# Attention values in one call and w_in cast on chip, in a pooled-attention and GELU-product kernel

## The chip, the cores and the metric

The kernel runs on one core of a Trainium2 chip. The time is the device time of one execution in microseconds (us). Before the change, four runs have a median of 287.18 us (287.03 to 288.27). TensorE does the matrix products, VectorE, ScalarE and GpSimd (POOL) work on elements, SyncE (SP) issues transfers.

## The reference, cut to what matters

```python
q, k, v: (8 batches, 8 heads, 576 tokens, 64) float32
k_p = k.reshape(B, H, 72, 8, D).mean(axis=3)      # pool 8 tokens into one
v_p = v.reshape(B, H, 72, 8, D).mean(axis=3)
attn = softmax(q @ k_p^T / sqrt(D))                # 576 x 72 for each head
x = (attn @ v_p), heads side by side               # 4608 tokens x 512
h = x @ w_in                                       # 512 x 2048
out = gelu_tanh(h) @ w_out                         # 2048 x 512
```

## The kernel before, in words

Tokens are worked on in nine groups: batches 0 to 6 with 512 tokens each, then the remainder R (the last 64 tokens of every batch, 512 in all), then batch 7. A group has two parts. Its **attention** pools k and v over eight tokens (`pool`, L147 to L149; `spread_v`, L169, lays v out in `vbd` by a mask), makes scores (L229, L236), exponentials on ScalarE (`exps`, L244), sums and norms (`norm`, L251 to L263, into `eb`), transposes the normed weights into `eT` by DMAs on SP's queue (`e_transpose_dma`, L293), and multiplies them with the values into a PSUM tile `xo`, which is cast to bf16 as `xT` (512 rows of x in four blocks ko of 128 partitions, 512 tokens wide). Its **mlp** is a first product `w_in_b` x `xT` (four products for each of 16 column blocks fo, `hidden`, L380; GELU by ScalarE into `gT`) and a second product.

The mlp of one group and the attention of the next run together: the mlp goes through its TensorE instructions in a written order, and a dictionary of hooks says ahead of which of them a piece of the next group's attention is put. The first product is steps 0 to 63, the second 64 to 175. For groups behind the first, the second product is done by seven block products instead of eight (L471 to L508): sums of blocks of gT (`g_sums`, L431 to L434, into `stage`) and of w_out (`w_sums`, tile `tw`), then 7 x 16 = 112 products of 256 columns in the order 1, 2, 6, 5, 7, 3, 4. The PSUM bank x takes part 1, then 6, 7 and 4 on top; its state after each is kept as k2, k0, and so on (`x_copy`, `x_add`). The order in which a schedule is written is the order on each engine; nothing is rearranged.

There are four ways to make values:

- `values_half` (L298), for batch 0: 256 tokens and two of four head pairs in a call.
- `values` (L313), for batch 1 and, in the changed kernel, for all later groups: all 512 tokens. For a batch it splits each product over partitions 0 to 127 into pieces that touch only the rows and the 64 columns of one head, first the eight SMALL ones on 32 rows, then the eight BIG ones on 64 rows (L325), which add onto the same PSUM. For R (L334) it is 64 products of 64 columns.
- `values_part` (L340), for the groups behind batch 1: 256 tokens in a call, sixteen products of 256 columns in both calls together (L348), or twice 32 of 64 columns for R (L356). Its two `xo` tiles hold two blocks ko each and are copied by ScalarE and VectorE (128x512 each, L88 and L90). The first call is at step 64 + 92 of the mlp before, the second at step 4 of the group's own mlp (counted in full-size steps).
- Because of the two halves, the first four column blocks of those mlps are done in products of 256 columns, half of the tokens after the other (`hidden_half`, L391, GELU L393).

PSUM is split in two tags, "mm" with four banks and "sc" with two tiles of two banks (scores, values).

At the start, SP's queue carries k, q and v of batch 0 (L539 to L546), and `load_w_in` (L549) loads w_in in four DMAs on POOL's queue, which turn float32 into bf16 on the way: columns 0 to 1023 behind the exponentials of batch 0, the rest behind `spread_v`. A one-element DMA on SP's queue (L643) reads the second of these pieces, so that what follows on SP (k, q of batch 1, w_out in float32 to `w_out_s` and `stage`, v of batch 1; L644 to L653) comes behind it. w_out is cast by POOL and ScalarE (`cast_w_out`). `mlp_first` (L511) is batch 0's mlp: it begins with the first 256 tokens (half 0) of column blocks 0 to 7, has the last transposes of batch 0 as hooks at 16 and 28 (`first_t`, L289) and the values of the second 256 tokens at 32 (`first_v`, L304), and ends with a plain second product (`output`, L396).

Of the kernel before, what the change touches and what calls it, by code (L numbers as in the profile page):

```python
# [8 lines left out]
F32 = mybir.dt.float32  # L9
# [10 lines left out]
def kernel(  # L20
# [21 lines left out]
    nc = tc.nc  # L42
# [43 lines left out]
    def copy(eng, out, in_):  # L86
        if eng is nc.scalar:
            eng.copy(out=out, in_=in_)  # L88
        else:
            eng.tensor_copy(out=out, in_=in_)  # L90
# [221 lines left out]

    def values(g, eng):  # L313

# [21 lines left out]
        for i in range(2):  # L336
            copy(eng, st[g]["xT"].rearrange("p (y i) t -> p i y t", i=2)[:, i], xo[i])


    def values_part(g, half, engs):  # L340

        xo = [psum.tile([128, 2, 256], F32, name="xo", tag="sc", bufs=2) for _ in range(2)]
        eT = st[g]["eT"]
        for x in range(2):
            if g < B:
                for pr in (x, x + 2):
                    for y, (c, n) in enumerate(PARTS[pr]):
                        nc.tensor.matmul(out=xo[pr // 2][:, x, :], lhsT=vbd[:, g, n, :],  # L348
                                         rhs=eT[:, 2 * half:2 * half + 2, c, :], start=(y == 0), stop=(y == 1))
                continue  # L350
            for pr in (x, x + 2):
                for b in range(4 * half, 4 * half + 4):
                    p0 = 64 * (b % 2)
                    t0 = 64 * (b - 4 * half)
                    for y, (c, n) in enumerate(PARTS[pr]):
                        nc.tensor.matmul(out=xo[pr // 2][:, x, t0:t0 + 64], lhsT=vbd[:, b, n, :],  # L356
                                         rhs=eT[:, b // 2, c, p0:p0 + 64], start=(y == 0), stop=(y == 1))
        for k in range(2):
            copy(engs[k], st[g]["xT"][:, 2 * k:2 * k + 2, 256 * half:256 * half + 256], xo[k])

# [74 lines left out]

    def mlp(g, hooks, last, split):
        hook = runner(hooks)
        if split:
            for half in range(2):
                for fo in (0, 2):  # L440
                    hidden_half(g, fo, half, lambda s: hook(s // 2) if s % 2 == 0 else None, 16 * half + 4 * fo)
        for fo in range(4 if split else 0, FO):
            hidden(g, fo, hook, 4 * fo)
# [30 lines left out]
        for n, (prod, acc, fresh) in enumerate([(1, xs, 1), (2, y, 1), (6, xs, 0), (5, z, 1), (7, xs, 0), (3, z, 0), (4, xs, 0)]):  # L474
# [17 lines left out]
            if prod == 1:  # L492
                x_copy(nc.vector, k2)
            elif prod == 6:
                x_copy(nc.scalar, k0)
            elif prod == 5:
                copy(nc.scalar, k1, z)
                add(out=k2, in0=y, in1=k2, op=ALU.add)
            elif prod == 7:
                x_add(k1, k1)  # L500
                if last:
                    store_pair(g, 1, osb[1], HN, DM)
            elif prod == 3:
# [101 lines left out]
    for j in range(2):  # L605
        scores(0, j)
        exps(0, j)
    load_w_in(0)
    load_w_in(1)
    pool(0, 5, 7)  # L610
# [5 lines left out]
    spread_v(0, nc.gpsimd, (2,))  # L616
    load_w_in(2)
    load_w_in(3)
# [12 lines left out]
    nc.scalar.preload_act_table_set(GELU_SET)  # L631
    norm(0, 2, nc.vector)
    norm(0, 3, nc.vector)

    def first_t(j):
# [6 lines left out]

    nc.sync.dma_start(out=gate[0:1], in_=w_in_b[0:1, 0, 512:513])  # L643
    kv_tile(1)  # L644
# [72 lines left out]
    for n_, g in enumerate(seq):  # L717
# [12 lines left out]
        if n_ + 1 < len(seq):  # L730
# [48 lines left out]
        if 2 <= n_ <= 5:  # L779
            at(hooks, 58, load_q, R, n_ - 2, n_ - 1, nc.sync)  # L780
        mlp(g, hooks, n_ + 1 == len(seq), n_ > 1)

# [29 lines left out]
```

## Time and profile before

| | |
|---|---|
| median of 4 runs | 287.18 us |
| profiled execution, its own time | 287.12 us |
| its span, first to last instruction | 285.4 us |
| granted TensorE clock | 1.00 |
| TensorE busy | 276.7 us, 97% |
| VectorE busy | 206.1 us, 72% |
| ScalarE busy | 166.7 us, 58% |
| POOL busy | 58.4 us, 20% |
| one pass of the main loop on TensorE (95.64 to 124.46) | 28.82 us |
| w_in, four DMAs of POOL, issued 9.58 to 16.34 | landed 15.53, 18.03, 21.49, 25.53 us |
| first product of batch 0 begins | 17.82 us |

The profile gives a busy time for each engine, the idle time in front of an instruction with what ended it, and a chain of waits followed back from the last instruction. Matrix products are pipelined: the time of one (0.38 us with 512 columns) is longer than the distance between two (0.216). A few records of TensorE are missing, so a gap of exactly one product is no wait.

### The profile page before, as it was taken

Reading aid. Unit: us, or ns where it says so; the run is one execution under the profiler, and the core shown is the slowest. Engines: PE = TensorE matmul, PEld = TensorE weight load, DVE = VectorE, ACT = ScalarE, POOL = GpSimd, SP = SyncE. Lnnn points to the kernel's source line nnn. Section 1 sums busy time; section 2 is a strip of 40 time slices with the busy share of each in tenths; the row PEclk is TensorE's granted clock in tenths of the full one; section 3 lists DMA queues with packets and bytes.
Section 4 is the critical chain, followed back from the end, with each engine's and each line's share of the span. In section 5 each row is a group of like instructions: output and inputs, shape, how many; then the busy total and the mean of one; then the engine's idle time right before and its main releaser. Section 6 shows DMA issues by size and latency. Waiting matters only on the chain.

```text
span 285.4 us, 5568 instructions
## 1 busy us (share of the span) xinstructions
PE 276.7 (97%) x2193; PEld 198.0 (69%) x2203; DVE 206.1 (72%) x377; ACT 166.7 (58%) x262; POOL 58.4 (20%) x91
## 2 busy tenths in 40 slices
PE   8889999999999999999999999999999999999994
PEld 3678854447884788478846984698468956985583
DVE  5882869989858985898589948994899345944521
ACT  1586574796457744775467547754785367536510
POOL 4730363003300340033003300331032100100000
PEclk9999999999999999999999999999999999999999
DMA  7999999999999997797979977936713530253003
GB/s 229 305 192 290 375 385 190 328 300 274 198 253 265 348 133 189 213 328 130 172 220 334 125 155 216 263 72 155 193 68 67 144 106 2 49 111 82 2 2 148
DMA packets 71357, 54.31 MB, mean 190 GB/s; under 512 B 45602, under 2 KB 57378, under 8 KB 71330
## 3 DMA queue, kind: packets, MB, share of 16 engines
q1 hardware_dynamic: 69218, 51.85, 70.7%
q0 software_dynamic: 2112, 2.10, 4.6%
q8 instruction: 17, 0.28, 0.4%
q14 instruction: 10, 0.08, 0.2%
HBM read 36.70 MB, written 9.44 MB: 162 GB/s over the span
## 4 chain that ended last, share of the span: by engine, by line
PE 82%; DMA 8%; DVE 7%; issue 1%; SPq 1%; POOL 0%; DVEq 0%
PE mm L485 32%; PE mm L380 29%; PE mm L391 10%; DMA w_out_s<-in_moe_w_out_dram 5%; PE xo L348 4%; PE x L485 2%; PE sc L229 2%; DMA kv<-in_v_dram 2%; DMA qT<-q_b 2%; DVE den L251 1%; DVE eb L263 1%; PE mm L396 1%; DVE kv L147 1%; DVE eb L278 1%; DVE kv L148 1%; PE xo L356 1%
## 5 line engine op out<-in xcount | busy, mean ns | idle before, releaser
L380 PE MATMUL mm<-xT,w_in_b 128*128 128x512 bf16 x392 | 87.4, 379 | 0.4
L382 ACT ACTIVATE gT<-mm 128x512 bf16<-128x512 f32 x100 | 59.7, 598 | 25.0 <-PE mm L380 24.9
L380 PEld LDWEIGHTS <-w_in_b 128*128 128x128 bf16 x400 | 39.1, 98 | 45.9 <-issue 0.3
L485 PEld LDWEIGHTS <-gT 128*128 128x128 bf16 x512 | 49.3, 98 | 7.1
L169 POOL TENSOR_TENSOR vbd<-kvb,vmask 128x256 bf16<-128x256 bf16 (+2 forms) x40 | 23.8, 616 | 92.6 <-DVE kvb L149 92.4
L391 PE MATMUL mm<-xT,w_in_b 128*128 128x256 bf16 x352 | 42.3, 273 | 0.1
L485 PEld LDWEIGHTS <-stage 128*128 128x128 bf16 x384 | 37.2, 98 | 4.2
L391 PEld LDWEIGHTS <-w_in_b 128*128 128x128 bf16 x352 | 34.1, 98 | 4.2 <-issue 0.2
L393 ACT ACTIVATE gT<-mm 128x512 bf16<-128x512 f32 x44 | 26.1, 597 | 14.7 <-PE mm L391 14.7
L90 DVE CAST xT<-xo 128x512 bf16<-128x512 f32 x16 | 11.1, 692 | 29.1 <-PE xo L348 23.5
L485 PE MATMUL mm<-w_out_b,gT 128*128 128x256 bf16 x240 | 30.8, 273 | 0.0
L244 ACT ACTIVATE e<-sc 128x576 f32<-128x576 f32 x36 | 22.5, 650 | 11.4 <-PE sc L229 6.6
L88 ACT COPY osb<-mm 128x512 f32<-128x512 f32 x23 | 13.5, 587 | 26.2 <-PE mm L485 26.2
L485 PE MATMUL mm<-tw,gT 128*128 128x256 bf16 x240 | 28.7, 273 | 0.0
L251 DVE TENSOR_REDUCE den<-e 128x8 f32<-128x576 f32 x36 | 26.4, 735 | 2.3 <-ACT e L244 2.3
L485 PE MATMUL mm<-tw,stage 128*128 128x256 bf16 x224 | 27.9, 273 | 0.0
L147 DVE TENSOR_TENSOR kv<-kv 128x1024 f32<-128x1024 f32 (+3 forms) x19 | 21.0, 1106 | 6.5 <-DMA kv<-in_k_dram 5.2
L431 DVE TENSOR_TENSOR stage<-gT 128x512 bf16<-128x512 bf16 (+1 forms) x31 | 16.2, 522 | 13.1 <-ACT gT L382 7.8
L88 ACT CAST xT<-xo 128x512 bf16<-128x512 f32 (+1 forms) x18 | 11.3, 634 | 18.9 <-PE xo L348 11.1
L263 DVE TENSOR_TENSOR eb<-e,r 128x576 bf16<-128x576 f32 x24 | 20.5, 855 | 0.8
L432 DVE TENSOR_TENSOR gT<-gT 128x512 bf16<-128x512 bf16 (+1 forms) x31 | 14.6, 470 | 6.6 <-ACT gT L382 5.1
L263 POOL TENSOR_TENSOR eb<-e,r 128x576 bf16<-128x576 f32 x6 | 6.9, 1151 | 52.6 <-ACT e L244 52.6
(84 smaller groups left out, 295.5 us busy)
## 6 DMA issues: line engine op xcount, KB each, us to landing
kv<-in_k_dram SPq DMA_DIRECT2D x7, 1024.0 KB, 6.9
q_sb<-in_q_dram SPq DMA_DIRECT2D x7, 1024.0 KB, 11.2
out_dram<-osb SPq DMA_DIRECT2D x13, 512.0 KB, 3.0
kv<-in_v_dram SPq DMA_DIRECT2D x6, 1024.0 KB, 8.9
kv<-in_v_dram SPq DMA_DIRECT2D x4, 512.0 KB, 10.1
w_in_b<-in_moe_w_in_dram POOLq DMA_DIRECT2D x4, 512.0 KB, 6.7
w_out_s<-in_moe_w_out_dram SPq DMA_DIRECT2D x2, 1024.0 KB, 13.5
stage<-in_moe_w_out_dram SPq DMA_DIRECT2D x2, 1024.0 KB, 14.5
```

Of the source, the lines that this page charges most:

```text
L88: eng.copy(out=out, in_=in_)
L147: add(out=t[:, :, 0:4, :], in0=t[:, :, 0:4, :], in1=t[:, :, 4:8, :], op=ALU.add)
L169: eng.tensor_tensor(out=vbd[p0:128, b, n0:n1, :].rearrange("p (c r) (hh d) -> p c (r hh) d", c=max(m, 1), d=D), in0=kvb[p0:128, 4 + c0:4 + ...
L244: nc.scalar.activation(out=e.rearrange("p (x h) s -> p x (h s)", x=2), in_=sc[:, :, 0:4 * Sp], func=ACT.Exp, scale=1.0 / 64.0)
L251: nc.vector.reduce_sum(out=den, in_=e, axis=AX.X)
L263: eng.tensor_tensor(out=o.rearrange("p (h s) -> p h s", s=Sp), in0=e, in1=r.unsqueeze(2).to_broadcast([128, H, Sp]), op=ALU.mult)
L380: nc.tensor.matmul(out=hp, lhsT=w_in_b[:, ko, fo * 128:(fo + 1) * 128], rhs=st[g]["xT"][:, ko, :], start=(i == 0), stop=(i == KO - 1))
L382: nc.scalar.activation(out=gT[:, fo, :], in_=hp, func=ACT.Gelu_apprx_tanh)
L391: nc.tensor.matmul(out=hp[:, f, :], lhsT=w_in_b[:, ko, (fo + f) * 128:(fo + f + 1) * 128], rhs=st[g]["xT"][:, ko, c0:c0 + 256], start=(ko ...
L393: nc.scalar.activation(out=gT[:, fo:fo + 2, c0:c0 + 256], in_=hp, func=ACT.Gelu_apprx_tanh)
L431: nc.vector.tensor_tensor(out=s3, in0=a11, in1=a21, op=ALU.subtract)
L485: nc.tensor.matmul(out=xs[p] if acc is xs else acc[:, p, :], lhsT=lt, rhs=rt, start=bool(fresh and m == 0 and (p == 0 or (last and acc is ...
```

## The change

It has four parts.

1. For batches 2 to 7 and R the two calls of `values_part` are gone. `values` is called once for all 512 tokens, at step 64 + 105 of the mlp before, and its two PSUM tiles are copied by ScalarE (blocks ko 0 and 2) and VectorE (blocks 1 and 3), 128x1024 each. For batch 1 both copies stay on ScalarE.
2. Those mlps no longer work in halves. Their first two column blocks are done by `hidden_two`, which takes the four products that need only the first copy ahead of the four others; the rest are `hidden`. This holds for batch 1's mlp too, which had no halves before.
3. The copy k2 after part 1 of the second product goes from VectorE to ScalarE.
4. w_in is loaded by eight DMAs of 512 KB in float32 on SP's queue, directly behind batch 0's last load, into a second kv buffer and `stage`. VectorE casts two pieces, POOL ten. The gate DMA is gone; w_out's loads wait for the casts that read their buffers.

```diff
-    def values(g, eng):
+    def values(g, engs):
...
         for i in range(2):
-            copy(eng, st[g]["xT"].rearrange("p (y i) t -> p i y t", i=2)[:, i], xo[i])
-
-
-    def values_part(g, half, engs):
...
+            copy(engs[i], st[g]["xT"].rearrange("p (y i) t -> p i y t", i=2)[:, i], xo[i])
...
+    def hidden_two(g, hook):
+
+        hp = [psum.tile([128, MAIN], F32, name="mm", tag="mm", bufs=4) for _ in range(2)]
+        for s, (f, ko) in enumerate([(0, 0), (0, 2), (1, 0), (1, 2), (0, 1), (0, 3), (1, 1), (1, 3)]):
+            hook(s)
+            nc.tensor.matmul(out=hp[f], lhsT=w_in_b[:, ko, f * 128:(f + 1) * 128], rhs=st[g]["xT"][:, ko, :],
+                             start=(ko == 0), stop=(ko == 3))
+        for f in range(2):
+            nc.scalar.activation(out=gT[:, f, :], in_=hp[f], func=ACT.Gelu_apprx_tanh)
+
+    def mlp(g, hooks, last):
         hook = runner(hooks)
-        if split:
-            for half in range(2):
-                for fo in (0, 2):
-                    hidden_half(g, fo, half, lambda s: hook(s // 2) if s % 2 == 0 else None, 16 * half + 4 * fo)
-        for fo in range(4 if split else 0, FO):
+        hidden_two(g, hook)
+        for fo in range(2, FO):
             hidden(g, fo, hook, 4 * fo)
...
             if prod == 1:
-                x_copy(nc.vector, k2)
+                x_copy(nc.scalar, k2)
...
     nc.scalar.preload_act_table_set(EXP_SET)
-
-    def load_w_in(c):
-        nc.gpsimd.dma_start(out=w_in_b[:, :, 512 * c:512 * c + 512],
-                            in_=moe_w_in[:, 512 * c:512 * c + 512].rearrange("(ko p) f -> p ko f", p=128))
+    w_in_s = []
+    for c in range(4):
+        if c % 2 == 0:
+            w_in_s.append(kvp.tile([128, KO, 1024], F32, name="w_in_s", tag="kv") if c == 0 else
+                      stage.rearrange("p (k f) -> p k f", k=KO))
+        o = 512 * (c % 2)
+        for k0 in (0, 2):
+            nc.sync.dma_start(
+                out=w_in_s[-1][:, k0:k0 + 2, o:o + 512],
+                in_=moe_w_in[128 * k0:128 * k0 + 256, 512 * c:512 * c + 512].rearrange("(ko p) f -> p ko f", p=128))
+
+    def cast_w_in(c, k0, eng, f0=0, f1=512):
+        o = 512 * (c % 2)
+        copy(eng, w_in_b[:, k0:k0 + 2, 512 * c + f0:512 * c + f1], w_in_s[c // 2][:, k0:k0 + 2, o + f0:o + f1])
...
     e_transpose_pe(0, 1, nc.vector, "mm")
+    cast_w_in(0, 2, nc.vector, 0, 256)
     scores(0, 2)
     exps(0, 2)
     for x in range(2):
         values_half(0, 0, x, [nc.vector, nc.scalar][x], "mm")
     scores(0, 3)
+    cast_w_in(0, 2, nc.vector, 256, 512)
     sums(0, 2)
     exps(0, 3)
     nc.scalar.preload_act_table_set(GELU_SET)
     norm(0, 2, nc.vector)
     norm(0, 3, nc.vector)
+    cast_w_in(0, 0, nc.gpsimd)
+    for c in range(1, 4):
+        cast_w_in(c, 0, nc.gpsimd)
+        cast_w_in(c, 2, nc.gpsimd, 0, 256)
+        cast_w_in(c, 2, nc.gpsimd, 256, 512)
...
-    nc.sync.dma_start(out=gate[0:1], in_=w_in_b[0:1, 0, 512:513])
...
-        at(hooks, va, values, n, nc.scalar)
+        at(hooks, va, values, n, [nc.scalar, nc.scalar])
...
-            at(hooks, 64 + 92, xT_tile, n)
-            at(hooks, 64 + 92, values_part, n, 0, [nc.scalar, nc.vector])
-        if n_ > 1:
-            at(hooks, 4, values_part, g, 1, [nc.scalar, nc.vector])
+            at(hooks, 64 + 105, xT_tile, n)
+            at(hooks, 64 + 105, values, n, [nc.scalar, nc.vector])
```

The calls of `load_w_in` are taken out as well; nothing else in the schedule moves.

More of the change, by code (lines that the diff above doesn't have):

```diff
@@ L336, in values @@
         for i in range(2):
-            copy(eng, st[g]["xT"].rearrange("p (y i) t -> p i y t", i=2)[:, i], xo[i])
-    def values_part(g, half, engs):
[L342 to L359, printed above, removed]
+            copy(engs[i], st[g]["xT"].rearrange("p (y i) t -> p i y t", i=2)[:, i], xo[i])
     def store(g, r, osb, c0=0, c1=DM, eng=nc.sync):
@@ L434, in g_sums @@
         nc.vector.tensor_tensor(out=s4, in0=a12, in1=s2, op=ALU.subtract)
-    def mlp(g, hooks, last, split):
-        hook = runner(hooks)
-        if split:
-            for half in range(2):
-                for fo in (0, 2):
-                    hidden_half(g, fo, half, lambda s: hook(s // 2) if s % 2 == 0 else None, 16 * half + 4 * fo)
-        for fo in range(4 if split else 0, FO):
+    def hidden_two(g, hook):
[7 more added lines that the diff above has]
+    def mlp(g, hooks, last):
+        hook = runner(hooks)
+        hidden_two(g, hook)
+        for fo in range(2, FO):
             hidden(g, fo, hook, 4 * fo)
@@ L607 @@
         exps(0, j)
-    load_w_in(0)
-    load_w_in(1)
     pool(0, 5, 7)
@@ L616 @@
     spread_v(0, nc.gpsimd, (2,))
-    load_w_in(2)
-    load_w_in(3)
     norm_two(0, 1, 5)
@@ L780 @@
             at(hooks, 58, load_q, R, n_ - 2, n_ - 1, nc.sync)
-        mlp(g, hooks, n_ + 1 == len(seq), n_ > 1)
+        mlp(g, hooks, n_ + 1 == len(seq))
 _INS = ['q', 'k', 'v', 'moe_w_in', 'moe_w_out']
```

## The prediction

> **What bounds the kernel.** I read the page first, its busy shares and its chain.
>
> ```profile
> PE 276.7 (97%) x2193; PEld 198.0 (69%) x2203; DVE 206.1 (72%) x377; ACT 166.7 (58%) x262; POOL 58.4 (20%) x91
> ...
> PE 82%; DMA 8%; DVE 7%; issue 1%; SPq 1%; POOL 0%; DVEq 0%
> ```
>
> TensorE works for 276.7 of 285.4 us, and 82% of the chain of work that ended last is TensorE. A change is worth what it takes from TensorE's order or adds to it; other engines count where they make TensorE wait. Then the chain in order of time, for one pass of the main loop (95.5 to 125 us; columns are start, length, piece):
>
> ```profile
> 106.68 0.87 PE xo L348 x8
> 107.55 2.18 PE mm L485 x20
> 109.74 0.87 PE mm L391 x8
> 110.61 0.87 PE xo L348 x8
> 111.48 2.62 PE mm L391 x24
> ```
>
> The values of a batch cost 2 x 0.87 us here: eight products of 256 columns between the second product's steps (L348), eight more inside the next first product. No piece waits. (The 112 products of a pass's second product are numbered 0 to 111.) A pass is 28.82 us (95.64 to 124.46, the same piece twice). The operation that replaces these rows runs once before, for batch 1 (timeline from 48.8 us; start, length, instruction, the wait before it):
>
> ```profile
> 49.01 1.81 PE L325 MATMUL xo<-eT,vbd 32*64 32x512 bf16 x16
> ...
> 50.65 1.93 ACT L88 CAST xT<-xo 128x1024 bf16<-128x1024 f32 x2 [4.30 <-PE xo L325]
> ...
> 50.75 1.47 PE L396 MATMUL mm<-w_out_b,gT 128*128 128x512 bf16 x6
> ```
>
> Sixteen products of 512 columns, on 32- and 64-row parts of the array, are over in 1.74 us (49.01 to 50.75) although they wait for vbd twice; full-size products of 512 columns pass at 0.216 us each (46 in 10.09 us), sixteen at 3.46. So the parts overlap.
>
> **1. Values in one call.** Taken one by one, the last four small products begin together but for one that waits until 49.86; the large ones begin in two groups of four at 50.19 and 50.41; TensorE goes on at 50.75. A group of four therefore costs 0.22, and each change of tile size adds about 0.1 (50.19 less 49.86 is 0.33; 50.75 less 50.41 is 0.34). Four groups at 0.22 and three changes at 0.1 are 1.2 us. Before: 16 x 0.109 = 1.74. Saving 0.54 in each of the six calls for batches 2 to 7 that move. If small groups of different i didn't overlap at 0.22 but at 0.33, 0.3 of it is lost. For the remainder (L356) count and width of the products stay: nothing. The first four column blocks of the first product go from 32 x 0.109 = 3.49 to 16 x 0.216 = 3.46: 0.03 in seven passes. The Trainium skill speaks against the change here: TensorEngine Tiling (Array Packing), Key Properties, says that a change of tiling mode drains TensorE. The rows have it at 0.1 a change; were each a full drain of the visible 0.4 us of such a product, the call would cost 2.1 and the sum be 5 us worse.
>
> **2. The new wait for xT.** Before, other products lie between a value product and its use. Now seven products of the second product remain behind the values (105 to 111): 7 x 0.109 = 0.76. The row of batch 1 gives the copy: ScalarE starts at 50.65, 0.1 before TensorE leaves the values, and two copies of 128x1024 take 1.93, one 1.01. First copy ready 0.97 after the values (with 0.06 to release), TensorE there after 0.76: **stall 0.21**. ScalarE has nothing ahead: table load at 104.26 to 105.54, next copy 107.37. The order (0,0), (0,2), (1,0), (1,2) gives 4 x 0.216 = 0.86 before the VectorE half is needed, at 1.83. VectorE has no copy of 128x1024 from PSUM; 256 elements take 0.42, 512 take 0.69, so 1.24 by the step (bounds 0.69 and 2 x 0.69). It starts 0.55 before ScalarE's end, hence is ready at 1.4 (1.6 at worst): hidden, cover 0.4. Ahead of it VectorE has the addition L504, which starts 0.25 after product 96 and takes 0.68, over before the values end. Behind it wait pool and k of the next batch, which before began 4 us after this point and now 3. The remainder has its first block done 0.93 earlier, no stall. In batch 1 the order removes a wait of 0.14 (52.63).
>
> Per pass: -0.54 - 0.03 + 0.21 = -0.36; times six is **-2.1**; remainder -0.03; batch 1 -0.14.
>
> **3. All four transposes of e at once.** Before, values at product 92 needed j = 0, 1, and j = 2, 3 only 3.9 us later. Now all four are needed at product 105: 106.52 + 13 x 0.109 = 107.94, or 136.76 one pass on. SP's timeline there, and the row of the tile eT (issue to landing):
>
> ```profile
> 129.38 5.99 SPq L293 DMA_TRANSPOSE eT<-eb  x4
> ```
>
> ```profile
> DMA to landing us min/median/max: 2.6/2.6/3.0
> ```
>
> The last of the four is issued at 134.15; with 2.6 it lands at 136.75, right at the edge. What decides is the copy of k2, which leaves VectorE (timeline from 126 us):
>
> ```profile
> 126.95 0.68 DVE L90 COPY osb<-mm 128x512 f32<-128x512 f32 x1
> 127.55 0.74 DVE L251 TENSOR_REDUCE den<-e 128x8 f32<-128x576 f32 x1
> ```
>
> Sums of j = 0 start at 127.55, but the exponentials are done at 127.1, and work ahead of the copy ends at 127.0. So the chain (sum, reciprocal, norm, three more) moves 0.44 forward, and with it the transposes, as SP has no other work in between. Margin 0.44; in the pass at 72 us the last lands at 79.66, 0.5 earlier 79.15, needed 79.0. I charge 0.1 for the first passes together. On ScalarE, k2 (0.59) fits: exponentials end at 98.77, k2 would end at 99.36, product 6 overwrites x from 99.72, scores j = 2 come at 99.54. Cover 0.3; without it the excess is paid in each pass.
>
> **4. The start.** Four DMAs with cast on POOL's queue and the one-element gate go. Eight DMAs of 512 KB of f32 go on SP's queue behind q; their casts go to VectorE (2 of 512 elements, 0.43) and POOL (4 of 1024 at 1.04, 6 of 512 at 0.62). q lands at 13.26; w_out, in the same 2 KB rows, comes at 1024 KB in 2.70 (34.93 to 37.63). So 512 KB each 1.35 us after about 13.1: pieces of columns 0-511 at 14.4 and 15.8, the last at 24. VectorE wants its piece at 16.4, POOL at 15.5, TensorE starts at 17.82: no delay, cover 0.6. Before, the four landed at 15.53, 18.03, 21.49, 25.53; later columns are needed at 19.6, 23.2, 26.7 and cast by 19.8 (its second half is used at 20.5), 23.4, 25.7. Everything behind on SP (kv and q of batch 1, then w_out, which waits for the casts out of its buffers until 20 and 24 to 26) lands 1 to 1.7 earlier. POOL is through by 25.7; q of batch 1 and w_out, next on it, come at 30 and 33. That ends this stall of TensorE (0.39 by the starts, of which the timeline from 30 us lists 0.23):
>
> ```profile
> 35.65 0.81 PE L396 MATMUL mm<-w_out_b,gT 128*128 128x512 bf16 x3 [0.23 <-POOL w_out_b L90]
> ```
>
> Against it stands VectorE. Its second cast (0.43) stands ahead of sums j = 2, and the two norms behind (L263) meet POOL's casts. What that does (timeline from 37 us):
>
> ```profile
> 37.68 2.03 POOL L90 CAST w_out_b<-w_out_s 128x1024 bf16<-128x1024 f32 x2 [0.54 <-DMA w_out_s<-in_moe_w_out_dram]
> ...
> 38.81 1.50 DVE L263 TENSOR_TENSOR eb<-e,r 128x576 bf16<-128x576 f32 x1
> ...
> 41.25 0.76 DVE L263 TENSOR_TENSOR eb<-e,r 128x576 bf16<-128x576 f32 x1
> ```
>
> The same norm takes 0.76 alone and 1.50 beside POOL's casts. With casts at most 1.04 apart I take 0.3 of waiting for the cast and each norm: 0.43 + 0.3 in front of eb j = 2, 0.3 more for j = 3. TensorE wants both, in front of products 16 and 28, and first_v after: **+1.0** (bounds 0.45 with no meeting; 1.7 with both norms at 1.50). The Trainium skill, SBUF — State Buffer, Who interferes with whom, has GpSimd and a VectorE operation with two SBUF inputs exclude each other for a whole instruction; by that alone, up to 1.04 for each of three, the start would lose up to 3.1 instead of 1.0. The row agrees with waiting, and its 0.74 is what I use.
>
> At 49 us batch 1's values wait for vbd, the end of exponentials, four norms, pool and spread. That chain starts 1.0 later, but the norm of 1.50 above now runs after POOL's earlier casts: -0.74. So vbd comes +0.26; TensorE (1.0 - 0.39 = +0.61) is there before it either way. **Start: +0.26** (bounds -0.3 and +0.9).
>
> **The sum.** -2.1 - 0.03 - 0.14 + 0.1 + 0.26 = -1.9 us. The profiled execution took 287.12 with a span of 285.4; the median of four runs is 287.18, so the two agree. Prediction 285.2. This measurement tells a change from none at about 0.3%, 0.86 us.
>
> **Rivals.**
> *The transposes land late* (ends slower). Place: the first small value product of each pass, waiting for the fourth transpose. Longer landings are seen: 4.4 us (pass at 95 us, first of four, beside loads). Its 2.6 plus margin 0.44 is covered; beyond 3.4 us the wait exceeds the 0.36 gained. At 4.4 it is 1.35 late, six times 8.1: 293.3. For it: the window has no slack. Against: the fourth landed in 2.6 in every pass of the loop where it is recorded. 0.10.
> *The start eats the gain.* Both norms and the cast fully held, 1.7 instead of 1.0, and vbd not earlier (the norm still meets casts, +0.74): start +1.7 instead of 0.26, 286.6. For it: POOL casts 10 times in 10 us. Against: they wait for data in between. 0.14.
> *w_in late.* Loads cover 0.6. At 1.6 us per 512 KB, as q and v landed beside other traffic, the first pair lands at 16.3, just in time; if the queue holds it 2 us longer, TensorE starts 1.4 later, 286.6. Against: SP is free at 5.4, data are queued from then. 0.06.
> *More than I count.* Start at its good bound and no wait for xT: 285.2 - 0.56 - 1.26 = 283.4. 0.10.
> *The change doesn't overlap* (value parts one behind another, 3.46): +2.26 six times, 298.8. Row 49.01 excludes nearly all of it; part of the 0.10 of the first rival at most.
> Forecast, 284.4 to 286.2: 0.60.
>
> Faster (below 286.3): 0.60 + 0.10 and a fifth of the two middle ones, 0.74. Same (286.3 to 288.0): 0.15. Slower: 0.11. The range takes the good case at half, 283.9, and the start that eats the gain with small waits for transposes, 287.2.
>
> **What would show it.** Chain: values of a pass in one piece of about 1.2 us, no pieces of 256-column first product, a gap of 0.2 in front of the first product put down to ScalarE's copy; passes of 28.46. If the gap is put down to VectorE, the second copy is what I mis-sized. A gap in front of the values from a DMA on eT is the first rival. At the start, TensorE at first_v at 23.3 instead of 22.29, and norms of over 1 us. A first product after 18 us means w_in. Wrong altogether if passes stay at 28.8.

## The result and the profile after

| | before | after |
|---|---|---|
| median | 287.18 us (79 runs, 286.66 to 288.94) | 286.73 us (53 runs, 285.58 to 290.06) |
| ratio to before, 95% interval | | 0.9978 [0.9969, 0.9986] |
| profiled execution, its own time | 287.12 us | 287.41 us |
| its span | 285.4 us | 285.7 us |

The change gains 0.22% (0.63 us by the ratio), less than the 0.3% that the prediction gives as the least this measurement tells from none; 0.7% was forecast. One execution of after (290.06 us) and one of experiment 6 (576.0 us) were slow ones, and the ratios leave them out. The profiled execution of after lies 0.68 above its median, so its waits are probably larger than the usual ones. First the page of after: busy time, the instruction queue, and the chain that ended last, by engine and by line.

```profile
PE 273.3 (96%) x2074; PEld 178.8 (63%) x2091; DVE 203.4 (71%) x363; ACT 168.8 (59%) x264; POOL 62.5 (22%) x97
...
q8 instruction: 16, 0.26, 0.4%
...
PE 86%; DMA 7%; DVE 3%; SPq 2%; issue 1%
PE mm L359 32%; PE mm L471 30%; PE mm L420 5%; PE mm L375 5%; PE mm L370 4%; DMA w_in_s<-in_moe_w_in_dram 3%; PE xo L325 3%; DMA eT<-eb 3%; PE sc L229 3%; PE x L471 2%; DMA qT<-q_b 2%; DVE eb L263 1%; SPq L541 1%; DVE w_in_b L90 1%; SPq L108 1%
```

TensorE's busy time fell by 3.4 us and the span didn't. Two pieces stand in the chain that the prediction gave little room: 3% of the span on a transpose (`DMA eT<-eb`), and VectorE's norms (`eb L263`) and its cast (`w_in_b L90`) at the start. A pass without trouble, from the chain of after in order of time (start, length, piece):

```profile
137.49 1.11 PE xo L325 x16
138.60 0.87 PE mm L471 x7
139.47 0.03 issue
139.50 0.38 PE mm L420
```

The values cost 1.11 us in one piece. The last of the seven products behind them starts at 139.20, so the first product could start 0.109 later, at 139.31; it starts at 139.50, 0.19 late. The same chain two passes on:

```profile
191.16 3.55 DMA eT<-eb
194.71 0.14 issue
194.84 1.18 PE xo L325 x16
```

Here the last transpose, issued at 191.16, lands 3.55 later and TensorE stands idle for 0.53 in front of the values. There are three such waits: 0.55 (values at 108.97), 0.53 (194.84) and 0.84 (253.29). Where the time went, pass by pass (from the start of one second product to the next, in us of the span; the first row ends at the first scores of batch 2, so batch 1's first product, with its -0.14, lies in it):

| | before | after | difference | prediction |
|---|---|---|---|---|
| start, to the first scores of batch 2 | 66.94 | 67.84 | +0.90 | +0.12 |
| to 96 (a wait of 0.13 in before) | 28.70 | 28.19 | -0.51 | -0.36 |
| to 125 (wait 0.55) | 28.82 | 29.00 | +0.18 | -0.36 |
| to 153 | 28.83 | 28.44 | -0.38 | -0.36 |
| to 182 | 28.83 | 28.45 | -0.37 | -0.36 |
| to 211 (wait 0.53) | 28.82 | 28.98 | +0.16 | -0.36 |
| to 240, the remainder's values | 29.16 | 29.16 | 0.00 | -0.03 |
| to 269 (wait 0.84) | 28.83 | 29.29 | +0.46 | -0.36 |
| the rest | 16.47 | 16.35 | -0.12 | 0 |
| sum | 285.4 | 285.7 | +0.3 | -1.9 |

(The sum of the last column has 0.1 for the transposes; its terms are -1.97, put down as -1.9.) Two terms of the sum are off in this execution: the start by 0.8, and three waits of 1.92 together in place of 0.1. The row to 96 is 0.15 better than forecast because before, too, waited there for a transpose: it landed at 77.56, and the values began 0.13 late, at 77.69.

**What makes the transposes late.** Traffic of the DMA engines in 40 slices of 0.1 us, after, from 191 us (the row of GB/s, the instruction queue, and the transposes' median from issue to landing):

```profile
GB/s 51 187 218 223 212 202 223 190 100 23 8 166 0 31 131 205 223 189 210 179 100 26 8 10 10 8 10 8 10 151 132 0 0 0 0 0 0 0 0 0
...
q8 instruction: 1, 0.02, 1.6%
...
eT<-eb SPq DMA_TRANSPOSE x2, 4.0
```

And the pass that doesn't wait, from 133 us:

```profile
GB/s 233 210 218 212 223 195 80 10 0 0 0 33 164 220 233 200 228 210 200 131 21 0 0 0 18 136 218 225 207 228 212 205 157 34 0 0 0 0 0 0
...
eT<-eb SPq DMA_TRANSPOSE x2, 2.6
```

A transpose moves for 0.9 us at about 200 GB/s and is over. In the first window the traffic falls behind 193.1 to 8 to 10 GB/s for 0.7 us, then a last piece goes, and the transposes land after 4.0 (median) instead of 2.6. What is there and not in the second window is a 16 KB transfer of the instruction queue: it starts at 192.13 (the slice of 166 GB/s) and takes 1.02, to 193.15. The thin tail begins as it ends, and its rate is about a twentieth of the full one. I read this so: one of the 16 DMA engines was held by the transfer and works off its share alone, and a transpose isn't landed until its last share is. (The trace doesn't name the engine of a packet, so this reading of the rates and times is not shown.) There are 16 such transfers in the span, for 2074 + 2091 TensorE instructions, one in 260. The Trainium skill, Runtime: NRT & Kernel Launch, Instruction fetch mechanics, says that an engine's instructions are refilled in blocks of 16 KiB, 256 of them, over a DMA queue of its own, and that the cost of crossing such a block is mostly hidden. Size and spacing agree with the rows here; the cost here falls on another transfer.

In the three passes of after that wait they start at 104.59, 192.13 and 250.67, beside the later transposes. In the passes at 195 and 253 the third and the fourth land late (4.25 to 4.64 and 3.55 to 3.80). In the pass at 109 the second and the third do (4.35 and 3.56); SP issues the fourth 1.0 later than in other passes, and it lands in 2.57. A fourth pass is hit as well, the remainder's (a transfer at 220.79; 4.49 and 3.63), but the first of its products that reads the last block comes 0.35 behind its first one, and it waits only 0.05. The traces of all 14 runs say the same of the loop (passes behind 60 us, fourth transposes whose landing is recorded): 37 had a transfer between issue and landing and took 2.84 to 4.06 us, 3.53 in the median; 54 had none and took 2.58 to 3.01, 2.60 in the median.

The trace of before had such transfers too. Its window from 133 us:

```profile
GB/s 223 215 215 185 56 2 0 0 76 213 221 219 205 205 152 21 0 0 12 279 201 207 209 182 68 4 0 0 0 0 6 8 8 10 8 10 35 195 0 0
...
q8 instruction: 1, 0.02, 1.8%
```

The same picture in slices of 0.125 us: a transfer from 135.39 to 136.81, then the thin tail of 8 to 10 GB/s to 137.5, for a transpose issued at 134.15. It cost nothing there, since the second half of the values began at 139.27. The change took that cover away. (The old cover wasn't complete: in the profile of experiment 2, with values in two calls, a transfer of 2.04 us at 103.94 lies beside the first two transposes, which take 6.09 and 4.52, and the values at 107.94 wait 0.65, probably for them.)

**The start.** The chain of after from 17 us (it stands for this execution, see experiments 2 and 6):

```profile
17.56 1.22 DVE w_in_b L90
...
19.71 0.90 DVE eb L263
...
21.54 1.46 DVE eb L263
...
24.09 1.03 PE xo L304 x8
```

VectorE sets the end here: its cast took 1.29 (timeline; 0.41 alone), the norms 0.90 and 1.45 (0.76 alone). TensorE waits 1.16 and 0.79 for them, and `first_v` is at 24.09 instead of 22.29. POOL's side of it, from the timeline (start, length):

```profile
17.46 1.04 POOL L90 CAST w_in_b<-w_in_s 128x1024 bf16<-128x1024 f32 x1 [0.78 <-DMA w_in_s<-in_moe_w_in_dram]
```

POOL's cast began at 17.46, VectorE's at 17.49; VectorE ended at 18.78, 0.28 behind POOL's end. The norm at 21.54 stands behind a cast of POOL from 21.34 in the same way.

### The profile page after: what moved, and what is told of

It reads as the page before. It is cut to its first block, busy times and chain, and to the rows that moved or that the text cites. A ratio compares the mean times of both kernels' runs of the same rounds, so it can differ in the third digit from the quotient of the medians.

```text
span 285.7 us, 5348 instructions
## 1 busy us (share of the span) xinstructions
PE 273.3 (96%) x2074; PEld 178.8 (63%) x2091; DVE 203.4 (71%) x363; ACT 168.8 (59%) x264; POOL 62.5 (22%) x97
## 4 chain that ended last, share of the span: by engine, by line
PE 86%; DMA 7%; DVE 3%; SPq 2%; issue 1%
PE mm L359 32%; PE mm L471 30%; PE mm L420 5%; PE mm L375 5%; PE mm L370 4%; DMA w_in_s<-in_moe_w_in_dram 3%; PE xo L325 3%; DMA eT<-eb 3%; PE sc L229 3%; PE x L471 2%; DMA qT<-q_b 2%; DVE eb L263 1%; SPq L541 1%; DVE w_in_b L90 1%; SPq L108 1%
## 5 line engine op out<-in xcount | busy, mean ns | idle before, releaser
L359 PE MATMUL mm<-xT,w_in_b 128*128 128x512 bf16 x440 | 97.6, 379 | 0.4
L361 ACT ACTIVATE gT<-mm 128x512 bf16<-128x512 f32 x112 | 66.9, 598 | 27.8 <-PE mm L359 27.7
L359 PEld LDWEIGHTS <-w_in_b 128*128 128x128 bf16 x448 | 43.8, 98 | 52.9
L471 PE MATMUL mm<-tw,gT 128*128 128x256 bf16 x240 | 29.9, 273 | 0.0
L88 ACT CAST xT<-xo 128x1024 bf16<-128x1024 f32 (+1 forms) x11 | 10.2, 935 | 31.4 <-PE xo L325 27.0
L88 ACT COPY osb<-mm 128x512 f32<-128x512 f32 x30 | 17.6, 588 | 15.2 <-PE mm L471 13.6
L263 DVE TENSOR_TENSOR eb<-e,r 128x576 bf16<-128x576 f32 x24 | 20.6, 859 | 0.8
L90 DVE CAST xT<-xo 128x1024 bf16<-128x1024 f32 (+1 forms) x9 | 9.9, 1105 | 13.3 <-PE xo L325 10.4
L263 POOL TENSOR_TENSOR eb<-e,r 128x576 bf16<-128x576 f32 x6 | 6.9, 1151 | 50.4 <-ACT e L244 26.9
L90 POOL CAST q_b<-q_sb 128x1024 bf16<-128x1024 f32 (+1 forms) x13 | 13.6, 1065 | 11.5 <-DMA q_sb<-in_q_dram 11.5
L370 PE MATMUL mm<-xT,w_in_b 128*128 128x256 bf16 x128 | 15.6, 273 | 0.2 <-DVE xT L90 0.2
L471 PE MATMUL mm<-w_out_b,stage 128*128 128x256 bf16 x128 | 15.3, 273 | 0.0
```

The costliest lines, as they stand in the source:

```text
L263: eng.tensor_tensor(out=o.rearrange("p (h s) -> p h s", s=Sp), in0=e, in1=r.unsqueeze(2).to_broadcast([128, H, Sp]), op=ALU.mult)
L359: nc.tensor.matmul(out=hp, lhsT=w_in_b[:, ko, fo * 128:(fo + 1) * 128], rhs=st[g]["xT"][:, ko, :], start=(i == 0), stop=(i == KO - 1))
L361: nc.scalar.activation(out=gT[:, fo, :], in_=hp, func=ACT.Gelu_apprx_tanh)
L370: nc.tensor.matmul(out=hp[:, f, :], lhsT=w_in_b[:, ko, (fo + f) * 128:(fo + f + 1) * 128], rhs=st[g]["xT"][:, ko, c0:c0 + 256], start=(ko ...
L471: nc.tensor.matmul(out=xs[p] if acc is xs else acc[:, p, :], lhsT=lt, rhs=rt, start=bool(fresh and m == 0 and (p == 0 or (last and acc is ...
```

## The experiments

The theory (A) is that the forecast's terms hold but for two: the start costs about 0.9, and the waits for eT come on top. For the waits there are two theories: B, the instruction transfers hit the last transposes in some passes; and its rival, that the margin of the transposes is simply too small. Ratios are to before, timed on the same chip.

**1. The value parts without the loading part** (parts 1 to 3 of the change).

```diff
-    w_in_s = []
...
-    cast_w_in(0, 2, nc.vector, 0, 256)
...
+    load_w_in(0)
+    load_w_in(1)
...
+    nc.sync.dma_start(out=gate[0:1], in_=w_in_b[0:1, 0, 512:513])
```

That is, w_in is loaded and gated as before.

> The change without its fourth part: w_in comes in by the four casting DMAs of POOL's queue and the gate, as before; values, first product and k2 as in the changed kernel. Theory (A: the start costs 0.9 us because VectorE and POOL hold each other up over the casts; B: each pass gains 0.36, less a wait of about 0.5 to 0.8 where a 16 KB instruction transfer falls on the last transposes of e): the start is that of before, TensorE reaches the scores of the first pass at 66.8 instead of 67.8; time 286.73 - 0.9 = 285.8, against before -0.5%. Rival (the passes give nothing, and w_in on SP's queue is neutral): 286.7 to 287.2.

Measured: 286.08 us, ratio 0.9967 [0.9944, 0.9990]; profiled 285.76. The start is that of before (`first_v` 22.30, first scores of batch 2 at 66.82). Waits for eT: 0.25 (79.2), 0.37 (193.34), 0.62 (251.54), together 1.24; the instruction transfers of the last two start at 190.69 and 248.55, 2.3 and 2.4 ahead of where the values would stand. So these parts gain about 1.0, where the prediction's terms for them give -2.17; the 1.24 is about the difference. The wait at 79.2 is of another kind: a transfer at 73.14 lies beside the first two transposes there, but the last one lands in an ordinary 2.65. It is the pass whose last transpose the prediction had landing 0.15 late.

**2. The loading part alone.**

```diff
-    load_w_in(0)
-    load_w_in(1)
...
+    w_in_s = []
...
+    cast_w_in(0, 2, nc.vector, 0, 256)
...
-    nc.sync.dma_start(out=gate[0:1], in_=w_in_b[0:1, 0, 512:513])
```

That is the kernel before with the whole of part 4.

> The kernel before with only the fourth part: w_in by SP's queue in float32, cast by VectorE and POOL. Theory A: first scores of the first pass at 67.9 to 68.0 instead of 66.94 (0.9 of the changed kernel and the 0.14 that its other order in batch 1's first product saves), passes of 28.82; 288.2. Prediction on record: +0.26 at the start, 287.4. Rival (the load itself, not the casts, is late): a gap of TensorE in front of the first product with w_in's DMA as its end, not in front of the transposes of e.

Measured: 287.48 us, ratio 1.0010 [0.9991, 1.0028]; profiled 288.42, where the first scores of batch 2 come at 67.85, +0.91, as in after. The median is 0.4 above before, half of that; the ratio gives 0.3 and its interval ends at 0.8. That is nearer the forecast's +0.26 than the theory's 0.9; this profile is of the longest of the twelve executions. The product of the two ratios, 0.9967 x 1.0010, is 0.9977, and after has 0.9978: the parts add up. VectorE's timeline of this execution, then POOL's (x3: three casts in one row):

```profile
17.48 0.41 DVE L90 CAST w_in_b<-w_in_s 128x512 bf16<-128x512 f32 x1
```

```profile
17.46 3.04 POOL L90 CAST w_in_b<-w_in_s 128x1024 bf16<-128x1024 f32 x3 [0.79 <-DMA w_in_s<-in_moe_w_in_dram]
```

The same two instructions 0.02 apart, and here VectorE went first: its cast took 0.41 and POOL's first cast 1.33. The next norm (18.82) paid instead, 1.20. `first_v` is at 22.81, and the rest of the loss comes later, at 33.35, where TensorE waits 0.5 for k of batch 1 (landed 29.40; 27.92 before).

**3. k2 back on VectorE.**

```diff
-                x_copy(nc.scalar, k2)
+                x_copy(nc.vector, k2)
```

> The changed kernel with the copy k2 back on VectorE. Point 3 of the prediction (the copy sets the chain of sums and norms back by 0.44, and the last transpose has that much to spare): passes without a 16 KB transfer now wait 0 to 0.1 in front of the values, the passes at 109, 195 and 253 us wait 0.44 longer each: 1.3 to 1.7 more than the changed kernel's 286.7, 288.2. Rival (ScalarE's copy was free but bought nothing, since SP's issue of 1.3 us each is the chain): the waits stay, 286.7.

Measured: 288.63 us, ratio 1.0038 [1.0019, 1.0057], 1.9 above after (286.73; 1.7 by the ratios). Waits for eT in seven passes: 0.49, 0.79, 0, 0.03, 0.92, 0.52 (remainder), 0.91, together 1.7 more than in after. Moving k2 is what makes room for the transposes, as the prediction had it.

**4. More TensorE instructions ahead of everything**: 36 narrow warm-up products for 12 wide ones.

```diff
-    warm_up(12, "mm")
+            nc.tensor.matmul(out=warm[:, 0:128], lhsT=zeros, rhs=zeros, start=True, stop=True)
...
+    warm_small(36, "mm")
```

> The changed kernel with 36 small products (128 columns) in the warm-up instead of 12 of 512: 48 instructions more on TensorE's queue, the same time on it. Theory B: a 16 KB transfer of the instruction queue comes every 256 instructions, so all of them move some 3 us ahead of the work; those at 104.6, 192.1 and 250.7 leave the window of the last two transposes, and the waits in front of the values at 109, 195 and 253 (0.55, 0.53, 0.84) go or move to passes where a transfer now falls: 285.4 to 286.0. Rival (the last transpose has no slack whatever runs beside it): the same three passes wait as before, 286.7.

Measured: 286.98 us, ratio 0.9987 [0.9969, 1.0005]. The transfers moved to 102.76, 188.99 and 246.98, and the waits from 0.55, 0.53, 0.84 to 0.28, 0.53, 0.13 (and 0.22 at 80.53). The wait at 195.11 is now that of the second transpose, which the transfer hit so that SP issued the third 0.95 later. Two of the three waits shrank as B says; the time is the rival's, not B's, and the start was 0.33 later. Not a clean test.

**5. VectorE's second cast on ScalarE.**

```diff
-    cast_w_in(0, 2, nc.vector, 256, 512)
...
     exps(0, 2)
+    cast_w_in(0, 2, nc.scalar, 256, 512)
```

> The changed kernel with VectorE's second cast of w_in (columns 256 to 511, upper two blocks) given to ScalarE, behind the exponentials of j = 2. Theory A: the sums of j = 2 begin at 17.7 again instead of 18.7, the norms fall where POOL waits for data, TensorE's waits of 1.16 and 0.79 in front of the transposes go almost wholly, and the start ends 0.3 to 0.5 ahead of before: 285.4 to 285.8. Rival (the norms are held up by POOL's casts wherever they stand): only the 0.4 of the cast itself is saved, 286.3.

Measured: 286.40 us, ratio 0.9972 [0.9953, 0.9990]. VectorE's timeline:

```profile
20.07 0.76 DVE L263 TENSOR_TENSOR eb<-e,r 128x576 bf16<-128x576 f32 x1
```

Both norms (18.38, and this one) take 0.76: they start as POOL's casts end (17.36 to 18.4, 18.73 to 20.17), and where the first meets one, POOL pays (0.89 for a cast of 0.61 at 18.73). TensorE no longer waits for the transposes; `first_v` is at 21.93, before 22.29. Yet the first scores of batch 2 are still 0.32 late: TensorE now waits 0.25 for a cast of w_in and 0.7 for k of batch 1 (landed 28.94). Against the profile of after that is 0.58 earlier, but the next experiment has two executions of the unchanged start that are earlier still (67.11 and 67.03). So what the move is worth behind `first_v` isn't shown; the time is the rival's 286.3, and the ratio isn't told apart from that of after.

**6. Values five products earlier, and five later** (after, place 100 and place 110).

```diff
-            at(hooks, 64 + 105, values, n, [nc.scalar, nc.vector])
+            at(hooks, 64 + 100, values, n, [nc.scalar, nc.vector])
```

> The changed kernel with the values at step 64 + 100 instead of 64 + 105: five more products behind them (0.55 us). The wait for ScalarE's copy (0.19 in six passes) goes, -1.15; the last transpose is needed 0.55 earlier: 0 to 0.1 in the three clean passes, 0.55 in the three that wait already. Sum +0.6: 286.7 to 287.5. Rival (the wait for the transposes is not set by when they are asked for): all six passes gain 0.19, 285.6.

> The changed kernel with the values at 64 + 110, two products behind them. The wait for the copy becomes 0.19 + 0.55 = 0.73 in six passes (+3.3); the waits for the transposes (0.55, 0.53, 0.84 in the profiled execution) fall to 0, 0 and 0.3 (-1.6): 288.0 to 288.6, with executions closer together, since what differs between them is the transposes. If the waits in front of the values stay, they are not the transposes'.

Measured: 288.45 us, ratio 1.0046 [1.0024, 1.0068], and 288.55 (eleven executions), ratio 1.0048 [1.0030, 1.0065]. Chain of the first, then of the second, same pass:

```profile
105.53 2.60 DMA eT<-eb
...
108.22 1.18 PE xo L325 x16
```

```profile
109.71 1.02 ACT xT L88
...
110.78 0.38 PE mm L420
```

Earlier, the wait for xT is gone and the transposes are waited for in each batch's pass (0.48, 0.79, 0.12, 0.34, 1.07, 1.07; remainder 0.87), though four of the six last ones land in 2.59 to 2.77 (3.53 and 3.49 where a transfer comes). The time is 1.0 above the forecast's upper end. Later, eT is hidden but for 0.22 at one place, and ScalarE's copy is waited for, 0.74 in six passes, as forecast. The eleven executions at 110 lie within 0.75 of each other, those of after within 2.6; but those of before lie within 2.3, so it isn't shown that the wait for eT is what varies. Place 105 is near the best of this design, and both sides of it cost 1.7 to 1.8.

Up to the first scores of batch 2 the code of these two kernels is that of after, and it shows how much a start varies. In both profiles `first_v` is at 23.07, and the first scores of batch 2 come at 67.11 and 67.03, 0.17 and 0.09 behind before, where 0.12 was forecast. VectorE's cast lost time again (1.29 and 1.01), but its second norm took 0.76 and not 1.45. The profile of experiment 3, with the same start too, is like that of after (24.11 and 67.87).

**7. Without the loading part, the norm of j = 0 on POOL instead of j = 1.**

```diff
-                at(hooks, nj, norm, n, j, nc.gpsimd if j == 1 else nc.vector)
+                at(hooks, nj, norm, n, j, nc.gpsimd if j == 0 else nc.vector)
```

> The first of these runs (w_in as before, values in one call) with POOL making the norm of j = 0 instead of j = 1. SP issues the transposes in the order of j, 1.3 us each; the second no longer waits for POOL's 1.15 us norm. By the durations the last one is issued 0.4 us earlier. Theory B: the waits in front of the values (0.25, 0.37, 0.62 in that run's profile) fall by up to 0.4 each: 285.0 to 285.5. Rival (VectorE's own chain is as long): the same 286.1.

Measured: 286.15 us, ratio 0.9963 [0.9942, 0.9985], as without it, which is the rival's number. The small wait at 79 is gone, and in the passes without a late transfer the last transpose was issued 0.2 to 0.4 earlier against its place. But 0.45 (193.42) and 0.84 (251.88) stay: at 193 it was issued no earlier (189.93; 189.83 in experiment 1), at 251 0.2 earlier, and with the transfers at 190.45 and 248.70 it took 3.36 and 3.99. So the margin came where it wasn't needed.

**8. The clean test: 40 very narrow products in the first stage**, without the loading part.

```diff
+            nc.tensor.matmul(out=warm[:, 0:32], lhsT=zeros, rhs=zeros[:, 0:32], start=True, stop=True)
...
+    at(hooks, 72, warm_small, 40, "sc")
```

> The value-product parts without the loading part, plus 40 products of zeros with 32 columns in the first stage (80 more TensorE instructions, weight loads included); nothing else differs from the run without the loading part. Theory B (the 16 KB transfers of the instruction queue come once in 256 TensorE instructions and push the last transposes of eT): relative to the program, the transfers come 80 x 0.055 = about 4.4 us earlier. In the run without these products they start 2.3 and 2.4 before the value products of the passes whose value products start at 193 and 251 (waits 0.37 and 0.62) and 2.3 behind those of the pass at 136 (no wait). So the waits of the passes at 193 and 251 should be under 0.15, and a wait of 0.3 to 0.8 should appear in the pass at 136. Rival (those passes are late for a reason of their own: their loads, their buffers): the same two passes wait 0.3 to 0.7, the one at 136 does not. In time: 286.1 plus 40 x 0.05 to 0.07 = 2.0 to 2.8 for the products, less 0.4 to 0.6 for the waits: 287.6 to 288.5; by the rival 288.1 to 288.9.

Measured: 285.44 us, ratio 0.9943 [0.9929, 0.9958]. The chain around 136 us, and around 193:

```profile
133.01 3.72 DMA eT<-eb
...
136.81 1.18 PE xo L325 x16
```

```profile
188.97 4.80 PE mm L471 x44
193.78 1.11 PE xo L325 x16
```

The passes at 193 and 251 no longer wait, and the one at 136, which never waited in after, waits 0.67; the transfers are now at 134.28, 186.49 and 244.49. That is B and not its rival: the same code of a pass waits or doesn't, by where in the program the transfer falls. (It was 2.3 ahead of the values' place at 193 in experiment 1 and is 7.2 ahead now.) The time was misjudged: it is 2.2 below the forecast's lower end. The products cost 1.0 where they stand (27.33 to 28.33), but TensorE waited 0.85 for w_out behind them in experiment 1, and that wait is gone. By the first scores of batch 2, work that is pure waste cost 0.14 (66.96 for 66.82; other profiles with this start lie at 66.64 to 67.06), and the waits for eT are 0.84 in all, 1.24 before. The interval of the ratio overlaps that of experiment 1, so a gain isn't shown.

**9. Without the loading part, ScalarE's copy cut in two**, and the first products ordered to use the first half at once, values at 106.

```diff
-            copy(engs[i], st[g]["xT"].rearrange("p (y i) t -> p i y t", i=2)[:, i], xo[i])
+            for y in range(2):
+                copy(nc.scalar, st[g]["xT"][:, 2 * y], xo[0][:, y])
+            copy(nc.vector, st[g]["xT"].rearrange("p (y i) t -> p i y t", i=2)[:, 1], xo[1])
...
-        for s, (f, ko) in enumerate([(0, 0), (0, 2), (1, 0), (1, 2), (0, 1), (0, 3), (1, 1), (1, 3)]):
+        for s, (f, ko) in enumerate([(0, 0), (1, 0), (0, 2), (1, 2), (0, 1), (0, 3), (1, 1), (1, 3)]):
```

> The value-product parts without the loading part, with ScalarE's copy cut in two (groups 0 and 2 of xT, 128x512 each, 0.59 by the copies of that size), the first products in the order (0,0), (1,0), (0,2), (1,2), and the value products one place later (106). If the wait of 0.19 in front of the first product is ScalarE's copy, it is gone in all six passes: -1.14; the later place gives each wait for eT 0.11 more cover: -0.2 to -0.3 in all. Expected 284.6 to 285.1 against 286.1. Rival (the wait only moves to the second group, or to VectorE's copy, which lands 0.05 before it is needed now): 285.6 to 286.3, with a wait inside the first product's eight instructions.

Measured: **284.31 us**, ratio 0.9906 [0.9894, 0.9919], better than both kernels and 0.3 below the forecast. Its chain:

```profile
107.20 1.11 PE xo L325 x16
108.31 0.76 PE mm L476 x6
109.08 1.73 PE mm L425 x8
```

No gap is left: 107.20 + 1.11 = 108.31, and by the starts of the instructions the first product follows its six predecessors without delay. The 0.19 was ScalarE's copy in all six passes. Waits for eT of 0.24 (192.14) and 0.45 (249.97) remain.

**10. The same at 107, with the norm of j = 0 on POOL.**

```diff
-            at(hooks, 64 + 106, values, n, [nc.scalar, nc.vector])
+            at(hooks, 64 + 107, values, n, [nc.scalar, nc.vector])
```

> As the split copy, with the value products at 107 and the multiplication of j=0 instead of j=1 on GpSimd. One place later leaves 5 x 0.109 = 0.55 behind the value products: the first group's copy of 0.59, begun 0.16 before TensorE leaves the values, is ready at 0.48, the second group's at 1.09 is needed at 0.98: a wait of 0.1 in six passes (+0.6), and the waits for eT lose another 0.1 where they are (-0.2 to -0.3). Expected 284.8 to 285.4, no better than the split copy at 106. Rival: the waits for eT are larger in the median execution than in the profiled one, then this one is the faster by 0.3 or more.

Measured: 284.66 us, ratio 0.9923 [0.9909, 0.9937]: no better than the ninth, as expected, and not told apart from it for certain (the intervals overlap). The forecast wait of 0.1 in the first product is 0.04. Its profile has waits for eT of 0.38 (79.46), 0.28 (192.95) and 0.61 (251.03).

**11. Without the loading part and without the order of the first two column blocks.**

```diff
-        hidden_two(g, hook)
-        for fo in range(2, FO):
+        for fo in range(FO):
```

> The value-product parts without the loading part and without the order of the first two groups of the first product: each group takes groups 0, 2, 1, 3 of xT in one run, as the rest of the product does. VectorE's half is then needed 0.43 behind the first product instead of 0.86. By the trace it lands 0.39 behind it (VectorE 196.08 + 1.23 = 197.31, first product 196.92), so the wait in front of it is 0 to 0.1 in six passes: 286.1 to 286.7. Rival (the copy lands later than its row shows, 0.06 to release and more under the locks): 0.3 to 0.4 each, 287.9 to 288.5.

Measured: 286.03 us, ratio 0.9964 [0.9952, 0.9976], the same as with it (286.08). The wait stays at 0.19, all in front of the first product. So the order that the change brings in part 2 bought nothing in these six passes: VectorE's copy is ready when it's needed without it. It bought 0.14 once, in batch 1, where both copies are on ScalarE: there the wait is back.

## Why the prediction was wrong, point by point

- **Values in one call, -0.54 each: right.** From place to place the call takes 1.21 us (1.11 in the chain, and 0.09 for the first change of tile size); 1.2 was forecast. A change adds 0.09 (0.088 to 0.094) to the 0.216 of the product before it, and groups of four follow each other at 0.24; the prediction's 0.22 comes from reading the second large group at 50.41, where it begins at 50.43. Undisturbed passes take 28.44 and 28.45; 28.46 was forecast.
- **The wait for xT, 0.21: right**, 0.19, and put down to ScalarE's copy. VectorE's copy takes 1.23 (1.24 forecast) and ends 0.47 before its half is needed (0.4 forecast); it is hidden without the order of the products, too (experiment 11).
- **k2 on ScalarE hidden, and what makes room for the transposes: right** (experiment 3, 1.7 to 1.9 us without it).
- **Transposes, +0.1: the step that failed.** The waits for eT are 1.92 in the profiled execution of after and 1.24 in that of experiment 1. I took 2.6 from issue to landing as the landing, from the passes "where it is recorded". The pass where the fourth transpose's landing is not recorded (129 to 140 in before) is the one that an instruction transfer hit; a missing record was read as an ordinary one. The 4.4 of the pass at 95 us, which the prediction put down to loads, has a transfer beside it as well (101.78, 1.49 us). The rival had the place right (first small product of a pass, waiting for the fourth transpose) and the wrong size and count: not six passes at 1.35, but three at 0.5 to 0.8. In place of an even 2.6 the runs showed 2.6 where no instruction transfer falls between issue and landing and 2.8 to 4.1 where one does; experiment 8 moved the transfers, and the waits went with them.
- **Start, +0.26: too small in some executions, not in others.** In the profiled one of after the term for the cast and two norms, +1.0 with a bound of 1.7, was +1.8 at `first_v`: 0.41 for the cast itself, 0.88 of waiting in it, 0.14 and 0.69 in the norms, less 0.2 by which VectorE was ahead. (The prediction's words have three waits of 0.3, its sum counts two.) The rest of the path was right. The norm that took 1.50 before takes 0.76:

```profile
40.61 0.76 DVE L263 TENSOR_TENSOR eb<-e,r 128x576 bf16<-128x576 f32 x1
...
50.91 0.10 PEld L325 LDWEIGHTS <-vbd 32*64 32x64 bf16 x1 [0.25 <-POOL vbd L169]
```

  So vbd comes 1.80 - 0.74 = 1.06 later by the sum and 1.04 by the trace (last piece ready at 50.85, 49.81 before), batch 1's values still wait for it, and with the -0.14 of batch 1 that makes the 0.90. With the same start, the profiles of experiment 6 have 0.17 and 0.09. By the ratios the loading part costs 0.3 (0.9978 against 0.9967 without it), as forecast. Which of the two engines loses a meeting differs between executions; why is open. The rival "the start eats the gain" had the first half right for the profiled execution (the cast and a norm held), not the second (vbd's norm wasn't).
- **w_out's stall gone, -0.39: right in size, wrong in reason.** "Everything behind on SP lands 1 to 1.7 earlier" didn't happen: k of batch 1 landed at 28.71 (27.92 before), q at 32.44 (31.72), w_out at 35.14 (34.93). The 4 MB of w_in in float32 stand ahead of them. The stall went because TensorE came 1.8 later.
- **The sum.** For the profiled execution, -1.97 + 0.78 (start) + 1.82 (transposes) - 0.15 (before's own wait at 77.69) - 0.12 (the end) is +0.36; +0.3 was measured. For the usual execution the ratio has -0.63, 1.3 worse than forecast. The waits for eT are enough for that: in the profiles of kernels with the values at this place (after, experiments 1, 4, 5 and 7) they add up to 1.2 to 1.9, where 0.1 was charged; experiment 8, with 0.84, has the lowest time of those at this place. How they divide in executions that weren't profiled is open. The upper end of the prediction's range, 287.2, is "the start that eats the gain with small waits for transposes", which describes the profiled execution in kind; its lower end, 283.9, is not half of the good case, which would be 284.3.

## What to carry to other kernels

Before a cover of some microseconds behind a DMA is given up, look at the landings that are late or missing in the trace, not at the median: in a program of some thousand instructions the small instruction queue is one of the transfers that compete. A wait that comes in some passes and not in others of the same code can point to something that counts instructions and not passes, and a handful of instructions that do nothing, put in front, tells it apart. A long copy in front of a product is better cut into the pieces that the first products need than hidden by a reordering of the products alone: the cut, with an order that uses its first piece at once, gained 0.19 in each pass, the order alone nothing in these passes. And one profile is one execution: before a loss that it shows is put down to the change, look for other runs with the same code at that place.

## What the runs showed of the hardware that was not expected

- An instruction transfer of 16 KB takes 0.9 to 2.0 us and, in after, lengthens a late transpose from 2.6 us to 3.5 to 4.6 from issue to landing; eighty more TensorE instructions ahead moved it by 4.9 us against the values at 193, and by 4.2 against those at 136 (2.3 behind them, then 1.9 ahead of their place).
- When POOL's cast and VectorE's of the same stretch start 0.02 to 0.03 us apart, POOL's first by the trace, either may win. VectorE lost in after (17.49, 1.29 us) and in the runs with k2 on VectorE (17.38, 1.29) and with values at 100 (17.19, 1.29), POOL in the loading part alone (1.33 for 1.04). The Trainium skill, SBUF — State Buffer, Who interferes with whom, has the two share a pair of ports that whoever issues first holds for a whole instruction, while the other is blocked; 1.29 against 0.41 for the same cast agrees, but the trace's own starts don't tell who was first.
- Products of 32 columns passed at about 0.025 us each (40 in 1.0).
